# Pacing the side work of a fused attention and FFN kernel: due times for matmul units, lone VectorE score tiles, zero fillers

## The chip, the cores and the metric

The kernel runs on one core of a Trainium2 chip. The metric is the device time of one execution in microseconds (us). The kernel before has a median of 885.13 us in 3 runs.

## The reference

The input x is 2048 x 640 in bfloat16. It is normalized to xn, and the output is x plus attention of xn plus a squared-ReLU feed-forward network of xn. Attention has 32 heads of 20 columns for q, and one k and one v for all of them.

```python
xn = (x - mean(x)) / sqrt(var(x) + 1e-5)
q = (xn @ wq).reshape(B, S, 32, 20); k = xn @ wk; v = xn @ wv
p = softmax(einsum("bhqd,bkd->bhqk", q, k) * 20 ** -0.5)
a = einsum("bhqk,bkd->bhqd", p, v).reshape(B, S, 640) @ wo
h = relu(xn @ w1 + b1) ** 2
out = x + a + h @ w2 + b2
```

## The kernel before, in words

**Blocks and tiles.** An opening of some 30 us loads x, normalizes and transposes it (xnT) and makes the first keys, values and queries. Then come 32 blocks: 4 query chunks of 512 rows (qc) times 8 groups of 4 heads (g). A block has 64 score tiles, 16 key tiles (kt) times 4 heads, each of 128 keys x 512 queries in one PSUM bank. The 2048 tiles are shared between two engines.

**ScalarE's tiles (ACT).** PE computes a score step (make_step, line 806): 3 tiles, then 2, then 3 again, into banks 0 to 2 and 3 to 4. The 4 heads lie on 4 groups of 32 rows of the PE array, so the matmuls of a step are row-tiled and run side by side. ACT takes the exponential of a whole step with one ACTIVATE (line 840). When the 4 heads of a key tile are done, a PV group of 4 column-tiled matmuls multiplies them with v into bank 6 (make_pv, line 850). A step waits for the ACTIVATE two steps back, since it takes over its banks.

**VectorE's tiles (DVE).** A set is one key tile with its 4 heads (new_set, line 902, takes the last unclaimed key tile of the block). Each head's scores go into bank 5 (make_dqk, line 919). DVE turns them into a number whose bits approximate the exponential (D1, line 956) and, once per set, makes a correction with W, U, T1 and T2 (lines 963 to 974) on 128 x 2048 elements; T2 of every second set runs on POOL in two halves (line 972). U writes ubuf, of which there is one, so U of a set waits for T2 of the set before. Three PV groups per set follow (make_dpv, line 864). In the kernel before, PE computes such a tile only straight behind a score step, if the planner has it ready within 0.05 us then.

**Misc units.** The rest of PE's work is cut into units that share bank 7, each with an evacuation on DVE: unit_QT (queries of a block), unit_FFN1 (128 hidden columns of a query chunk; DVE adds the bias and takes the maximum, POOL squares), unit_OUT (128 rows x 320 columns of the output of a finished query chunk: 12 groups of the second FFN matmul, 1 of the bias, 8 of the out-projection), and unit_OUTP, the same for the last chunk without the last 2 head groups. Each step of a unit is a group of 4 column-tiled matmuls (col4, line 576). The list misc (lines 744 to 771) gives their order.

**The planner.** The order on every engine is fixed while the program is built (the loop at lines 993 to 1106). It knows a planned duration and the inputs of each operation, and takes again and again the one that can start first; among those that start within 0.03 us the lower number of priority goes first: on PE 0 for a score step, 1 for PV, 2 for a misc unit. A misc unit is taken from the first six of the list as soon as its inputs are planned (lines 1037 to 1042). On the chip each engine works its list in this order and waits for semaphores. The planner keeps DVE's double-speed operations and POOL's apart in time (lock).

**The end.** After the loop PE adds the last two head groups for the last chunk (tail_mm, line 1118), DVE adds the stored part (tail_ev, line 1127), and SP stores the rows.

Of the kernel before, what the change touches and what calls it, by code (L numbers as in the profile page):

```python
# [37 lines left out]
DLEAD = 14.0  # L38

# [49 lines left out]
class Op:  # L89
# [3 lines left out]
    def __init__(self, name, eng, dur, parts, deps=(), toks=(), lat=0.06, lock=False):  # L93
# [3 lines left out]
        self.lat, self.lock = lat, lock  # L97
# [14 lines left out]
def bass_parallel_sum__grouped_kv_mqa__dense_activation_squared_relu__prompt_kernel(nc, A_x, A_wq, A_wk, A_wv, A_wo, B_x, B_w1, B_b1, B_w2, B_b2, out):  # L112
    es = ExitStack()
    with es:
# [40 lines left out]
        part = sb("part", [128, 4, D], F32)  # L155
        scr = sb("scr", [128, 4], F32)
# [6 lines left out]
        ubuf = xfree[:, 4 * SETW:5 * SETW]  # L163
# [75 lines left out]
        v_vxpad = c_pool.n  # L239

# [349 lines left out]
        def unit_KT(c):  # L590
            sts = range(4 * c, 4 * c + 4)
            ch = [(0.21, (lambda dt=dt: col4(lambda j: wk_c[:, dt, :], xnT[:, dt, 512 * c:512 * (c + 1)], 512, dt, dt == DT - 1, DH))) for dt in range(DT)]
# [51 lines left out]
        def unit_FFN1(qc, f):  # L644
            sts = range(4 * qc, 4 * qc + 4)
            ch = [(0.21, (lambda dt=dt: col4(lambda j: w1_sb[:, dt, f * 128 + 32 * j:f * 128 + 32 * j + 32], xnT[:, dt, qc * 512:(qc + 1) * 512], 512, dt, dt == DT - 1)))
                  for dt in range(DT)]

            def evac(p):
# [11 lines left out]
                q = Op(f"SQ{qc}_{f}", "POOL", 1.05, [lambda e: e.tensor_tensor(out=h2T[:, qc % 2, f, :], in0=hT_tmp[:, k % 2, :], in1=hT_tmp[:, k % 2, :], op=ALU.mult)], dp, tk, lock=True)  # L661
# [20 lines left out]
        def out_chunks(mats, bank=MB, first=True, last=True):  # L682
            n = len(mats)
            ch = []
            for k, (l, r) in enumerate(mats):
                kk = k if first else k + 1
                ch.append((0.145, (lambda kk=kk, k=k, l=l, r=r: col4(lambda j: l[:, 32 * j:32 * j + 32], r, 320, kk, last and k == n - 1, 32, bank))))
# [39 lines left out]
        GP1 = G - 2  # L727
# [24 lines left out]
        misc.append(unit_B1())  # L752
        for qc in range(QC):
            ff = [unit_FFN1(qc, f) for f in range(FT)]
            oo = [unit_OUT(qc - 1, st, h) for st in range(4 * (qc - 1), 4 * qc) for h in range(2)] if qc >= 1 else []
            for g in range(G):
                b = qc * G + g
                if b + 2 < NBLK:
                    misc.append(unit_QT(b + 2))
                nf = min(2, len(ff)) if qc == QC - 1 else (FT * (g + 1)) // G - (FT * g) // G  # L760
                lst = ff[:nf]
                ff = ff[nf:]
                if qc < QC - 1:
                    misc += lst
                if oo:
                    misc.append(oo.pop(0))
                if qc == QC - 1:
                    misc += lst
        for st in range(4 * (QC - 1), ST):
            for h in range(2):  # L770
                misc.append(unit_OUTP(st, h))
# [34 lines left out]
        def make_step():  # L806
# [20 lines left out]
            st_["qk"] = Op(f"QK{j}", "PE", 0.31 if len(tl) < 3 else 0.33, parts, deps, toks, lat=0.2)  # L827
# [22 lines left out]
        def make_pv(b, kt):  # L850
# [11 lines left out]
            return Op(f"PV{b}_{kt}", "PE", 0.22, parts, deps, toks, lat=0.2)  # L862

        def make_dpv(s):
# [14 lines left out]
            return Op(f"DPV{b}_{kt}_{term}", "PE", 0.22, parts, deps, toks, lat=0.2)  # L879
# [39 lines left out]
        def make_dqk(heads):  # L919
# [16 lines left out]
            else:  # L936
                toks += all_pro
            return Op(f"DQK{d}", "PE", 0.06, [mm(ps[:, bank, :], kT[32 * h:32 * h + DH, kt * 128:(kt + 1) * 128], qT[32 * h:32 * h + DH, b % NQS, :], True, True, (32 * h, 0))],
                      deps, toks, lat=0.2), s, h, bank
# [7 lines left out]
        def after_dqk(o, s, h, bank):  # L947
# [8 lines left out]
            d1 = dv(f"D1_{n}_{i}", 0.66, lambda e: e.tensor_scalar(out=lbuf[:, a, cs].bitcast(U16), in0=ps[:, bank, :], scalar1=XA, scalar2=XB, op0=ALU.mult, op1=ALU.add),  # L956
# [36 lines left out]
        while True:  # L993
            best = {}

            def consider(eng, prio, op, ap):
# [5 lines left out]
                s = max(free[eng], r)  # L1002
                if op.lock:
                    s = max(s, lock_free[0])
                best.setdefault(eng, []).append((s, prio, op, ap))
# [57 lines left out]
            if pick is None:  # L1063
                break
            _, prio, o, ap = pick
# [52 lines left out]
        def tail_mm(k, g, first, last):  # L1118
# [4 lines left out]
            o = Op(f"OF{k}_{g}", "PE", 0.145, out_chunks(mats, bank, first, last)[0][1](), deps, lat=0.2)  # L1123
# [131 lines left out]
```

## Time and profile before

| | |
|---|---|
| median of 3 runs | 885.13 us (882.9 to 886.19) |
| the profiled execution's own time | 884.17 us |
| its span, first to last instruction | 882.4 us |
| busy: PE, DVE, ACT, POOL | 790.4, 658.4, 809.1, 251.3 us |
| mean granted clock of TensorE | 0.814 |

The median says how long the kernel takes; the rows of the trace all come from the one profiled execution, so sums are made against its 884.17 us, which is its span and 1.8 us around it. Busy time counts an engine's own instructions, and for PE the end of a matmul is modelled, since matmuls overlap. The granted clock is 1.0 at 2.4 GHz and 0.5 at 1.2 GHz.

### The profile page before, as it was taken

To read this page: it belongs to the slowest core of one execution; us is meant where nothing else is said; L and a number is where in the kernel's file an instruction comes from. 1 tells how busy PE (TensorE), PEld (TensorE's weight loads), DVE (VectorE), ACT (ScalarE), POOL (GpSimd) and SP (SyncE) were. 2 spreads that over 40 slices of the span, in tenths; PEclk is the share of its full clock that TensorE was granted. 3 is DMA by queue.
4 is the path that set the end of the run, shared out by engine and by line. 5 is a ranking of instruction groups with operands and counts; after the bars stand their busy time and mean duration, and the time that the engine had idled before them with its cause. 6 is when DMAs were issued, how large, how long until landed. Compare 5 with 4: busy or idle time off the path is not lost.

```text
span 882.4 us, 20648 instructions
## 1 busy us (share of the span) xinstructions
PE 790.4 (90%) x9319; PEld 239.7 (27%) x9319; DVE 658.4 (75%) x942; ACT 809.1 (92%) x732; POOL 251.3 (28%) x162
## 2 busy tenths in 40 slices
PE   7699988889899999988999989988889999978997
PEld 3222222111123333312114333321122333311333
DVE  6778887866668898886657887877586688875763
ACT  7599998998889999999889989999998999999895
POOL 3323433132113233522112332342121135221230
PEclk8689987655569999977559999986576999965799
DMA  9300000000000000000000000000000000000000
GB/s 322 84 1 2 1 1 1 1 1 1 1 2 16 17 16 3 16 1 1 1 1 16 18 1 17 16 2 1 1 1 1 17 17 17 16 1 1 2 2 32
DMA packets 11706, 14.81 MB, mean 17 GB/s; under 512 B 2017, under 2 KB 10978, under 8 KB 11618
## 3 DMA queue, kind: packets, MB, share of 16 engines
q1 hardware_dynamic: 10306, 13.44, 4.9%
q8 instruction: 73, 1.20, 0.5%
q10 hardware_dynamic: 1312, 0.05, 0.1%
q14 instruction: 15, 0.12, 0.0%
HBM read 10.87 MB, written 2.62 MB: 15 GB/s over the span
## 4 chain that ended last, share of the span: by engine, by line
PE 48%; ACT 42%; DVE 6%; issue 1%; DVEq 0%
PE ps L533 48%; ACT PT L840 42%; DVE x_sb L956 1%; DVE hT_tmp L652 1%; DVE Tn L890 1%; DVE qT L635 1%; DVE T L892 0%; DVE x_sb L965 0%; PE ps L581 0%; DVE out_sb L715 0%; DVE out_sb L1132 0%; DVE x_sb L963 0%; DVE part L734 0%; DVE OTn L896 0%; DVE tbuf L967 0%
## 5 line engine op out<-in xcount | busy, mean ns | idle before, releaser
L840 ACT ACTIVATE PT<-ps 128x1536 bf16<-128x1536 f32 (+1 forms) x685 | 788.6, 1265 | 57.1 <-PE ps L533 54.0
L533 PE MATMUL ps<-qT,kT 20*128 20x512 bf16 x2048 | 332.9, 458 | 63.2 <-ACT PT L840 55.2
L956 DVE TENSOR_SCALAR x_sb<-ps 128x512 uint16<-128x512 f32 x336 | 230.5, 686 | 140.8 <-PE ps L533 138.8
L972 POOL TENSOR_TENSOR tbuf<-tbuf,x_sb 128x1024 bf16<-128x1024 bf16 x84 | 178.8, 2151 | 435.5 <-DVE tbuf L967 435.5
L533 PE MATMUL ps<-PT,vx 128*32 128x512 bf16 x1712 | 201.6, 462 | 2.4 <-DVE Tn L890 2.4
L533 PEld LDWEIGHTS ps<-qT,kT 20*128 20x128 bf16 x2048 | 72.2, 94 | 343.5 <-ACT PT L840 251.5
L967 DVE TENSOR_TENSOR tbuf<-x_sb 128x2048 bf16<-128x2048 bf16 x84 | 103.7, 1235 | 1.4
L661 POOL TENSOR_TENSOR big<-hT_tmp 128x512 bf16<-128x512 bf16 x48 | 54.7, 1146 | 151.7 <-DVE hT_tmp L652 151.7
L533 PEld LDWEIGHTS ps<-PT,vx 128*32 128x32 bf16 x1712 | 45.0, 95 | 135.7 <-issue 129.0
L533 PE MATMUL ps<-xnT,w_sb 128*32 128x512 bf16 x960 | 74.8, 401 | 6.4 <-DVE qT L635 2.8
L533 PE MATMUL ps<-w_sb,big 128*32 128x320 bf16 x1536 | 75.5, 309 | 2.5 <-DVE part L734 0.8
L963 DVE TENSOR_SCALAR x_sb<-x_sb 128x2048 uint16<-128x2048 uint16 x84 | 69.3, 825 | 1.4
L965 DVE TENSOR_SCALAR x_sb<-x_sb 128x2048 uint16<-128x2048 uint16 x84 | 62.1, 740 | 0.0
L533 PE MATMUL ps<-xnT,wq_sb 128*20 128x512 bf16 x620 | 56.8, 473 | 1.1 <-DVE out_sb L715 0.6
L974 DVE TENSOR_TENSOR tbuf<-tbuf,x_sb 128x2048 bf16<-128x2048 bf16 x42 | 51.7, 1232 | 0.2
L533 PE MATMUL ps<-wo_pad,OTn 128*32 128x320 bf16 x1024 | 49.3, 300 | 0.7 <-DVE part L734 0.7
L533 PEld LDWEIGHTS ps<-w_sb,big 128*32 128x32 bf16 x1536 | 37.9, 98 | 28.5 <-issue 9.5
L652 DVE TENSOR_SCALAR hT_tmp<-ps,b1col 128x512 bf16<-128x512 f32 x48 | 35.8, 746 | 9.8 <-PE ps L533 8.8
L533 PE MATMUL ps<-x_sb,vx 128*32 128x512 bf16 x336 | 38.7, 450 | 2.6 <-DVE Tn L890 2.5
L533 PE MATMUL ps<-tbuf,vxc 128*32 128x512 bf16 x336 | 39.2, 456 | 0.3 <-POOL tbuf L972 0.2
L533 PE MATMUL ps<-x_sb,vxh 128*32 128x512 bf16 x336 | 38.8, 452 | 0.0
L635 DVE CAST qT<-ps 128x512 bf16<-128x512 f32 x31 | 21.2, 682 | 20.5 <-PE ps L533 20.2
(81 smaller groups left out, 315.2 us busy)
## 6 DMA issues: line engine op xcount, KB each, us to landing
w_sb<-in_B_w_dram SPq DMA_DIRECT2D x2, 1920.0 KB, 10.6
xr<-in_A_x_dram SPq DMA_DIRECT2D x16, 160.0 KB, 2.3
out_dram<-out_sb SPq DMA_DIRECT2D x16, 160.0 KB, 1.8
x_sb<-in_A_x_dram SPq DMA_DIRECT2D x3, 640.0 KB, 6.7
wq_sb<-in_A_wq_dram SPq DMA_DIRECT2D x1, 800.0 KB, 9.7
wo_pad<-in_A_wo_dram SPq DMA_DIRECT2D x4, 200.0 KB
x_sb<-in_A_x_dram SPq DMA_DIRECT2D x2, 320.0 KB, 3.5
wk_c<-in_A_wk_dram ACTq DMA_DIRECT2D x1, 25.0 KB, 3.2
```

Source lines behind the costliest of these rows:

```text
L533: return lambda e: e.matmul(out_, l, r, start=start, stop=stop, tile_position=tp)
L635: o = Op(f"QTe{b}", "DVE", 0.66, [lambda e: e.tensor_copy(out=qT[:, b % NQS, :], in_=ps[:, MB, :])], [p] + list(q_users.get(b - NQS, [])))
L652: o = Op(f"RL{qc}_{f}", "DVE", 0.75, [lambda e: e.tensor_scalar(out=hT_tmp[:, k % 2, :], in0=ps[:, MB, :], scalar1=b1col[:, f:f + 1], scal ...
L661: q = Op(f"SQ{qc}_{f}", "POOL", 1.05, [lambda e: e.tensor_tensor(out=h2T[:, qc % 2, f, :], in0=hT_tmp[:, k % 2, :], in1=hT_tmp[:, k % 2, : ...
L840: return Op(f"ACT{st_['j']}", "ACT", 0.064 + 0.4267 * n, [lambda e: e.activation(out=PT[:, s0:s0 + n, :], in_=ps[:, b0:b0 + n, :], func=AF ...
L890: tn = Op(f"TN{b}", "DVE", 0.72, [lambda e: e.transpose(out=Tn[:, a, :], in_=ps[:, PVB, :])], [lastpv, tm_op.get(b - 2)])
L956: d1 = dv(f"D1_{n}_{i}", 0.66, lambda e: e.tensor_scalar(out=lbuf[:, a, cs].bitcast(U16), in0=ps[:, bank, :], scalar1=XA, scalar2=XB, op0= ...
L963: s["wop"] = [dv(f"W{n}", 0.65, lambda e: e.tensor_scalar(out=W.bitcast(U16), in0=L.bitcast(U16), scalar1=0xFF80, scalar2=124, op0=ALU.bit ...
L965: s["uop"] = dv(f"U{n}", 0.65, lambda e: e.tensor_scalar(out=ubuf.bitcast(U16), in0=L.bitcast(U16), scalar1=0x7F, scalar2=0x3F80, op0=ALU. ...
L967: s["t1"] = [dv(f"T1_{n}", 1.17, lambda e: e.tensor_tensor(out=T, in0=L, in1=ubuf, op=ALU.mult), [s["uop"]] + ([("pv", old, 2)] if old els ...
L972: s["t2"].append(dv(f"T2_{n}", 2.1, lambda e, ks=ks: e.tensor_tensor(out=T[:, ks], in0=T[:, ks], in1=ubuf[:, ks], op=ALU.mult), s["t1"], 4 ...
L974: s["t2"].append(dv(f"T2_{n}", 1.17, lambda e: e.tensor_tensor(out=T, in0=T, in1=ubuf, op=ALU.mult), s["t1"], 4))
```

## The change

Units get a due time `at`, counted in blocks, and are taken only when the planner's progress has reached it: the opening's units at 0, the others spread by their cost over what is left of the 32 blocks, and QT of block b at b - 2 + 0.02. The planner charges 0.1 us when PE goes from row-tiled (mode R) to column-tiled (mode C) matmuls or back, and new durations: 0.215 us for a score step (0.31 to 0.33 before), for a PV and for each group of QT, KT and FFN1 (0.21 or 0.22 before), 0.14 for a group of OUT (0.145), 1.15 for a square (1.05). A DVE score tile may ride with a score step if it is ready within 0.1 us of it, and go alone if no score step can start within 0.5 us. While PE has a gap and has been planned busy for less than 0.7 of the time, it is given fillers: 4 matmuls with zero weights that add to bank 6. There are two ubufs, in a tensor of their own. OUTP leaves out 3 head groups instead of 2.

```diff
+DGAP = 0.5
+SWITCH = 0.1
+FILL = 0.7
...
+        zeros32 = sb("zeros32", [128, 32], BF16)
...
-        ubuf = xfree[:, 4 * SETW:5 * SETW]
+        ubuf = sb("ubuf", [128, 2, SETW], BF16)
...
+        add(P.pool, lambda e: e.memset(zeros32[:], 0.0), inc=c_pool)
+        v_zeros = c_pool.n
...
-        def commit(op):
-            s = max(free[op.eng], op.ready())
+        pe_mode = ["C"]
+
+        def start_of(op, r, switch=True):
+            s = max(free[op.eng], r)
+            if switch and op.eng == "PE" and op.mode != pe_mode[0]:
+                s = max(s, free["PE"] + SWITCH)
             if op.lock:
                 s = max(s, lock_free[0])
+            return s
+
+        def commit(op):
+            s = start_of(op, op.ready())
+            if op.eng == "PE":
+                pe_mode[0] = op.mode
...
-        GP1 = G - 2
+        GP1 = G - 3
...
+        for u in misc:
+            u.at = 0.0
+        others = []
         for qc in range(QC):
...
+            if qc == 0:
+                others += [(unit_FFN1(0, f), 0.3) for f in range(FT)] + [(unit_FFN1(1, f), 0.3) for f in range(FT)]
+            else:
+                others += [(unit_OUT(qc - 1, st, h), G * qc + 0.1) for st in range(4 * (qc - 1), 4 * qc) for h in range(2)]
+                if qc + 1 < QC:
+                    others += [(unit_FFN1(qc + 1, f), G * qc) for f in range(FT)]
+        others += [(unit_OUTP(st, h), NBLK - (G - GP1) + 0.1) for st in range(4 * (QC - 1), ST) for h in range(2)]
+        cost = [sum(c[0] for c in u.chunks) for u, _ in others]
+
+        left = sum(cost)
+        t = 0.3
+        for (u, t0), c in zip(others, cost):
+            t = max(t, t0)
+            u.at = t
+            t += c * (NBLK - 0.3 - t) / left
+            left -= c
+        for b in range(2, NBLK):
+            q = unit_QT(b)
+            q.at = b - 2 + 0.02
+            others.append((q, 0.0))
+        misc += [u for u, _ in sorted(others, key=lambda x: x[0].at)]
...
-            return Op(f"DQK{d}", "PE", 0.06, [mm(
+            return Op(f"DQK{d}", "PE", 0.02 if heads else 0.215, [mm(
...
-            s["uop"] = dv(f"U{n}", 0.65,
-                          s["d1"] + (sets[n - 1]["t2"] if n >= 1 else []), 4, True, x_read if n < 1 else ())
+            s["uop"] = dv(f"U{n}", 0.74,
+                          s["d1"] + (old["t2"] if old else []), 4, True, x_read if n < 2 else ())
...
+        credit = [0.0, 0.0]
+
+        def pe_credit(t):
+            credit[1] = min(credit[1] - FILL * (t - credit[0]), 0.6)
+            credit[0] = t
+            return credit[1]
...
-                if rd is not None and rd <= free["PE"] + 0.05:
+                if rd is not None and heads[0] and rd <= free["PE"] + 0.1:
                     best["PE"] = [(max(free["PE"], rd), -1, r[0], ("dqk",) + r[1:])]
                 else:
-                    heads[0] = None
+                    heads[0] = []
+                    if r is not None:
+                        r[0].dur = 0.215
+                    nq = pend[0]["qk"].ready() if pend[0] is not None else None
+                    if rd is not None and (nq is None or nq > max(free["PE"], rd) + DGAP):
+                        consider("PE", 3, r[0], ("dqk",) + r[1:])
...
+                progress = cur["b"] + 1.0 - len(unclaimed[cur["b"]]) / KT
                 for u in misc[:6]:
-                    if u.can():
+                    if u.at <= progress and u.can():
...
+            if pick[2].eng == "PE":
+                while pick[0] > free["PE"] + 0.1 + (0.2 if pick[2].mode == "R" and pe_mode[0] == "R" else 0.0) and pv_blk[0] < NBLK and pv_blk[0] in pv_begun and pe_credit(free["PE"]) < 0.0:
+                    f_ = Op("fill", "PE", 0.215, [mm(ps[32 * jj:32 * jj + 32, PVB, :], zeros32[:, :], kT[:, 0:512], False, False, (0, 32 * jj)) for jj in range(4)])
+                    commit(f_)
+                    credit[1] += f_.dur
+                pe_credit(max(pick[0], free["PE"]))
+                credit[1] += pick[2].dur
...
-            tail_mm(k, G - 2, True, False)
+            for g in range(GP1, G - 1):
+                tail_mm(k, g, g == GP1, False)
```

The planned durations of D1, W, U and T1 go from 0.66, 0.65, 0.65 and 1.17 to 0.686, 0.74, 0.74 and 1.235 us, of T2 from 1.17 to 1.235 (2.1 to 2.15 for a half on POOL).

## Rows read from the trace of the kernel before

**Rows 1.** The page: busy times, granted clock in 40 slices, chain that ended last.
```profile
PE 790.4 (90%) x9319; PEld 239.7 (27%) x9319; DVE 658.4 (75%) x942; ACT 809.1 (92%) x732; POOL 251.3 (28%) x162
...
PEclk8689987655569999977559999986576999965799
...
PE 48%; ACT 42%; DVE 6%; issue 1%; DVEq 0%
```

**Rows 2.** Stretches: us, busy (count) of PE, PEld, DVE, ACT, POOL; granted clock, DMA.
```profile
60.00:120.00 60.00, 54.65 (x686) 16.01 (x690) 52.81 (x73) 59.44 (x53) 22.93 (x17) 1.00 0.01 2
120.00:280.00 160.00, 142.16 (x1237) 34.06 (x1229) 114.34 (x155) 141.15 (x123) 39.04 (x21) 0.66 0.01 2
280.00:380.00 100.00, 92.94 (x1397) 33.08 (x1395) 88.10 (x122) 99.35 (x88) 37.14 (x22) 1.00 0.04 13
380.00:480.00 100.00, 90.16 (x828) 22.21 (x824) 64.45 (x92) 91.89 (x81) 23.11 (x12) 0.66 0.00 1
480.00:580.00 100.00, 91.96 (x1365) 31.90 (x1357) 85.24 (x118) 96.43 (x85) 32.47 (x19) 0.98 0.05 15
580.00:680.00 100.00, 89.06 (x775) 20.84 (x771) 72.11 (x100) 90.54 (x79) 25.17 (x14) 0.66 0.00 1
680.00:780.00 100.00, 93.35 (x1423) 33.76 (x1419) 81.29 (x116) 98.43 (x86) 30.24 (x18) 0.98 0.05 15
780.00:840.00 60.00, 54.50 (x491) 13.34 (x487) 39.22 (x54) 55.60 (x49) 13.30 (x7) 0.60 0.00 1
840.00:872.00 32.00, 30.47 (x553) 13.06 (x553) 14.59 (x23) 31.34 (x28) 5.46 (x3) 1.00 0.01 3
...
40.00:872.00 832.00, 758.18 (x8920) 224.00 (x8920) 624.93 (x865) 781.77 (x680) 234.14 (x134) 0.81 0.02 6
```

**Rows 3.** Groups by line, 280 to 380 us: count, busy us, mean ns, idle before.
```profile
L956 DVE TENSOR_SCALAR x_sb<-ps 128x512 uint16<-128x512 f32 x46 | 31.5, 685 | 7.2 <-PE ps L533 7.0
...
L533 PE MATMUL ps<-PT,vx 128*32 128x512 bf16 x220 | 22.0, 389 | 0.8 <-DVE Tn L890 0.8
```

**Rows 4.** The same view, 190 to 230 us.
```profile
L533 PE MATMUL ps<-PT,vx 128*32 128x512 bf16 x72 | 11.1, 607 | 0.3 <-DVE Tn L890 0.3
L956 DVE TENSOR_SCALAR x_sb<-ps 128x512 uint16<-128x512 f32 x14 | 9.6, 689 | 10.3 <-PE ps L533 10.1
```

**Rows 5.** Groups of the whole span, from the page.
```profile
L840 ACT ACTIVATE PT<-ps 128x1536 bf16<-128x1536 f32 (+1 forms) x685 | 788.6, 1265 | 57.1 <-PE ps L533 54.0
...
L956 DVE TENSOR_SCALAR x_sb<-ps 128x512 uint16<-128x512 f32 x336 | 230.5, 686 | 140.8 <-PE ps L533 138.8
...
L967 DVE TENSOR_TENSOR tbuf<-x_sb 128x2048 bf16<-128x2048 bf16 x84 | 103.7, 1235 | 1.4
...
L963 DVE TENSOR_SCALAR x_sb<-x_sb 128x2048 uint16<-128x2048 uint16 x84 | 69.3, 825 | 1.4
L965 DVE TENSOR_SCALAR x_sb<-x_sb 128x2048 uint16<-128x2048 uint16 x84 | 62.1, 740 | 0.0
```

**Rows 6.** Timeline of PE: start us, length us, instructions merged.
```profile
80.45 1.26 PE L533 MATMUL ps<-xnT,w_sb 128*32 128x512 bf16 x20
81.64 0.39 PE L533 MATMUL ps<-qT,kT 20*128 20x512 bf16 x3
81.96 0.40 PE L533 MATMUL ps<-PT,vx 128*32 128x512 bf16 x4
...
855.29 1.13 PE L533 MATMUL ps<-w_sb,big 128*32 128x320 bf16 x28
```

**Rows 7.** Instructions on tile hT_tmp: ns min/median/max, first and last start.
```profile
L248 PE MATMUL ps<-hT_tmp,ones_bf x22: 379/380/634, 1.5 to 8.0; 128*128 128x512 bf16 x22
```

**Rows 8.** Timeline of POOL in the opening.
```profile
9.57 1.74 POOL L301 TENSOR_SCALAR big<-x_sb,rstd,nmr 128x640 bf16<-128x640 bf16 x2 [6.52 <-DVE nmr L294]
```

**Rows 9.** Timeline of the end.
```profile
875.07 0.45 DVE L734 TENSOR_TENSOR part<-ps,xr 128x320 f32<-128x320 f32 x1
...
876.90 3.28 DVE L1132 TENSOR_TENSOR out_sb<-ps,part 128x320 bf16<-128x320 f32 x8 [1.38 <-PE ps L533]
```

More of the change, by code (lines that the diff above doesn't have):

```diff
@@ L89, with __init__ @@
 class Op:
-    def __init__(self, name, eng, dur, parts, deps=(), toks=(), lat=0.06, lock=False):
+    def __init__(self, name, eng, dur, parts, deps=(), toks=(), lat=0.06, lock=False, mode="C"):
         self.name, self.eng, self.dur, self.parts = name, eng, dur, parts
@@ L96, in __init__ @@
         self.toks = list(toks)
-        self.lat, self.lock = lat, lock
+        self.lat, self.lock, self.mode = lat, lock, mode
         self.start = self.fin = None
@@ L591, in unit_KT @@
             sts = range(4 * c, 4 * c + 4)
-            ch = [(0.21, (lambda dt=dt: col4(lambda j: wk_c[:, dt, :], xnT[:, dt, 512 * c:512 * (c + 1)], 512, dt, dt == DT - 1, DH))) for dt in range(DT)]
+            ch = [(0.215, (lambda dt=dt: col4(lambda j: wk_c[:, dt, :], xnT[:, dt, 512 * c:512 * (c + 1)], 512, dt, dt == DT - 1, DH))) for dt in range(DT)]
             def evac(p):
@@ L660, in evac @@
                     dp += dp2
-                q = Op(f"SQ{qc}_{f}", "POOL", 1.05, [lambda e: e.tensor_tensor(out=h2T[:, qc % 2, f, :], in0=hT_tmp[:, k % 2, :], in1=hT_tmp[:, k % 2, :], op=ALU.mult)], dp, tk, lock=True)
+                q = Op(f"SQ{qc}_{f}", "POOL", 1.15, [lambda e: e.tensor_tensor(out=h2T[:, qc % 2, f, :], in0=hT_tmp[:, k % 2, :], in1=hT_tmp[:, k % 2, :], op=ALU.mult)], dp, tk, lock=True)
                 ffn_sq.append(q)
@@ L686, in out_chunks @@
                 kk = k if first else k + 1
-                ch.append((0.145, (lambda kk=kk, k=k, l=l, r=r: col4(lambda j: l[:, 32 * j:32 * j + 32], r, 320, kk, last and k == n - 1, 32, bank))))
+                ch.append((0.14, (lambda kk=kk, k=k, l=l, r=r: col4(lambda j: l[:, 32 * j:32 * j + 32], r, 320, kk, last and k == n - 1, 32, bank))))
             return ch
@@ L752, in bass_parallel_sum__grouped_kv_mqa__dense_activation_squared_relu__prompt_kernel @@
         misc.append(unit_B1())
+        for u in misc:
+            u.at = 0.0
+        others = []
         for qc in range(QC):
[L754 to L771, printed above, removed]
+            if qc == 0:
[18 more added lines that the diff above has]
+        misc += [u for u, _ in sorted(others, key=lambda x: x[0].at)]
         unclaimed = [list(range(KT)) for _ in range(NBLK)]
@@ L826, in make_step @@
                 toks += all_pro
-            st_["qk"] = Op(f"QK{j}", "PE", 0.31 if len(tl) < 3 else 0.33, parts, deps, toks, lat=0.2)
+            st_["qk"] = Op(f"QK{j}", "PE", 0.215, parts, deps, toks, lat=0.2, mode="R")
             for (b, kt, h) in tl:
@@ L937, in make_dqk @@
                 toks += all_pro
-            return Op(f"DQK{d}", "PE", 0.06, [mm(ps[:, bank, :], kT[32 * h:32 * h + DH, kt * 128:(kt + 1) * 128], qT[32 * h:32 * h + DH, b % NQS, :], True, True, (32 * h, 0))],
-                      deps, toks, lat=0.2), s, h, bank
+            return Op(f"DQK{d}", "PE", 0.02 if heads else 0.215, [mm(ps[:, bank, :], kT[32 * h:32 * h + DH, kt * 128:(kt + 1) * 128], qT[32 * h:32 * h + DH, b % NQS, :], True, True, (32 * h, 0))],
+                      deps, toks, lat=0.2, mode="R"), s, h, bank
         def dv(name, dur, fn, deps, prio, lock=True, toks=(), eng="DVE"):
@@ L955, in after_dqk @@
             old = sets[n - 2] if n >= 2 else None
-            d1 = dv(f"D1_{n}_{i}", 0.66, lambda e: e.tensor_scalar(out=lbuf[:, a, cs].bitcast(U16), in0=ps[:, bank, :], scalar1=XA, scalar2=XB, op0=ALU.mult, op1=ALU.add),
+            d1 = dv(f"D1_{n}_{i}", 0.686, lambda e: e.tensor_scalar(out=lbuf[:, a, cs].bitcast(U16), in0=ps[:, bank, :], scalar1=XA, scalar2=XB, op0=ALU.mult, op1=ALU.add),
                     [o] + ([old["pv"][0], old["t1"][0], old["uop"], old["wop"][0]] if old else []), 1, False, x_read if n < 2 else ())
@@ L1001, in consider @@
                     return
[L1002 to L1005, printed above, removed]
+                best.setdefault(eng, []).append((start_of(op, r, False), prio, op, ap))
             if act_next < len(steps) and steps[act_next]["qk"].fin is not None and act_can(steps[act_next]):
@@ L1122, in tail_mm @@
             deps = [tb_op[(qc, g)], part_ev[(st, h)]] + (bank_free[bank] if first else [])
-            o = Op(f"OF{k}_{g}", "PE", 0.145, out_chunks(mats, bank, first, last)[0][1](), deps, lat=0.2)
+            o = Op(f"OF{k}_{g}", "PE", 0.14, out_chunks(mats, bank, first, last)[0][1](), deps, lat=0.2)
             commit(o)
@@ L1141, in bass_parallel_sum__grouped_kv_mqa__dense_activation_squared_relu__prompt_kernel @@
         for k in range(7):
-            tail_mm(k, G - 2, True, False)
+            for g in range(GP1, G - 1):
+                tail_mm(k, g, g == GP1, False)
         for k in range(8):
             if k == 7:
-                tail_mm(k, G - 2, True, False)
+                for g in range(GP1, G - 1):
+                    tail_mm(k, g, g == GP1, False)
             p = tail_mm(k, G - 1, False, True)
```

22 lines of the change are left out of this document (11 added, 11 removed).

## The prediction

> **What bounds the kernel now.** The page first. ScalarE (ACT) is busy 92% of the span and PE 90%, and the chain that ended last is made of these two, 48% and 42%. PE's share is modelled, so the next thing to see is the line of the granted clock: it is not steady, it swings four times between 9 and 5 tenths [rows 1].
>
> The stretches show what the swing means. In four of them (60 to 120, 280 to 380, 480 to 580, 680 to 780 us, 360 us together) the clock is 0.98 to 1.00, that is 2.4 GHz, and PE has some 11 to 14 matmuls per us. ACT is idle there for 0.56, 0.65, 3.57 and 1.57 us, 6.35 us or 1.8%. In the four between (420 us) the clock averages 0.60 to 0.66 with about 8 matmuls per us, and ACT is idle for 18.85, 8.11, 9.46 and 4.40 us, 40.82 us or 9.7% [rows 2]. That is 41 of all 57.1 us that line 840 sat idle, nearly all of it until a PE matmul ended [rows 5].
>
> The groups of one dense and one thin stretch show why: a PV matmul takes 389 ns in the first and 607 in the second, which is the same work at 1.2 GHz [rows 3, 4]. What differs is the misc units. The list is taken greedily, so the out-projection and FFN1 units of a query chunk are used up in its first half, and the second half has little but score and PV matmuls. PE does less per us, the clock falls, and what is left takes so long that ACT waits.
>
> VectorE (DVE) has room: 624.93 of the 832 us from 40 to 872, but 88.10 of 100 in the best dense stretch [rows 2]. It waits most before L956, the first step of a score tile: 7.2 us of 100 in the dense stretch, 10.3 of 40 in the thin one, both for PE [rows 3, 4]. So ACT bounds the dense stretches, and PE at the low clock delays ACT in the thin ones.
>
> **The sum, part by part**, against the profiled execution's own 884.17 us, 0.96 under the median of the runs.
>
> A. **Pacing and fillers keep the clock up.** FFN1, OUT and OUTP units, and QT from block 2, get due times spread by cost over the 32 blocks. Four kinds of work are moved with them: their matmuls, evacuations on DVE, the squares on POOL, and the loads and stores on SP; each slot has blocks, not us, before its next use, so nothing waits for them. If the thin 420 us idle like the dense 360, their 40.82 us become 7.4: **-33.4**. Bounds: 0 if the clock does as before, -42 if all 780 us idle like 280 to 380 (0.65%). I take 1.8% because the new mix is nearest to the four dense stretches together.
>
> The PE load supports this. A column-tiled group of 4 matmuls costs 0.215 us at the high clock: five take 1.26, the last 0.40, so four starts cover 0.86. A 320-column group costs (1.13 - 0.175) / 7 = 0.137, the 0.175 being what one group outlasts its slot (0.39 - 0.215). After a score step the next mode starts 0.32 us on, 0.105 over the slot [rows 6]. With 672 score steps, 420 PV, 276 DVE-PV, 155 QT, 10 KT and 240 FFN1 groups (counts from the loops, with 8 more sets, below), 672 of the 320-column ones and, an assumption, 120 score tiles that go alone: 1893 x 0.215 + 672 x 0.137 = 499 us. Two switches for each of 792 row-tiled steps are 166. Fillers, to 0.7 of 782 us, add 48, about 225 of them. That is 713 of 782 us, 91%. The stretch 280 to 380, by the same account (88 score steps with 265 matmuls, 163 groups of 512 columns and 120 of 320, which make its 1397 matmuls [rows 2]), has 37 + 35 + 16 = 89%, and ACT idles 0.65% there. I take **0** for the fillers; bounds 0 and, if a quarter of the 225 delay ACT by a whole slot, +12.
>
> Do fillers with zero weights count for the clock? The warm-up matmuls have a moving operand of zeros, and among those 22 the length falls from 634 to 380 ns [rows 7]. So I take it that zeros count.
>
> B. **More DVE sets.** A set of 4 tiles costs DVE 4 x 0.686 + 0.825 + 0.740 + 1.235 and half as much again of a T2 like T1, together 6.16 us, and spares ACT 4 x 788.6 / 1712 = 1.84 us, the 1712 being 2048 less the 336 of L956 [rows 5]. A score tile may now go alone when the next step is over 0.5 us off, and the second ubuf frees U from the T2 of the set before, which POOL may still be working on. I take the best dense share, 0.881, from 40 to 790 us, with the last 32 us before the end as they are (14.59): 661 against 624.93 - 14.59 = 610 [rows 2], 51 us more, 8 sets: **-14.7**. Bounds: the planner charges 6.1 us for a set where it charged 5.7, so in the same planned time 5 sets fewer, +9; DVE at 0.95, 16 sets more, -30. Each D-PV group is counted above; L956 takes the bank before PE can refill it, as now.
>
> C. **The end.** The last part is evacuated at 875.07, and only then do the last 64 out-projection matmuls run, with the first result at 876.90 [rows 9]. OUTP units are now due from 3 blocks before the end, and lack one group more. Groups 5 and 6 are then ready while DVE normalizes the last block, and behind OTn, which DVE has done just before 875.07, stand only 0.14 of matmul, its latency (some 0.4) and the evacuations, so the first comes at about 875.6: **-1.3**. Bounds: +1.1 (8 groups more in line) and -2.
>
> D. **The rest at 0.** The memset of zeros32 on POOL lies in the 6.52 us that POOL waits for nmr [rows 8]; without that cover it is less than one of the two operations of that row, 0.9 us. Planner durations alter only the order. The wait moved to the older T2 is met earlier, so what stands behind U on DVE comes no later.
>
> Sum: 884.17 - 33.4 - 14.7 - 1.3 = 834.8, and with the 0.96 to the median **836 us**. What is late next is ACT itself, nearly full.
>
> **The rule on switching.** In rows 6 PV starts 0.32 us after the score step, whose matmuls are recorded for 0.39: the next mode starts before the former has ended, and a switch costs 0.105. The Trainium skill (TensorEngine Tiling (Array Packing), section Tiling Modes) says that changing the tiling mode drains TensorE. A full drain would by that rule cost 0.175 here, PE would need 547 + 1584 x 0.175 = 824 us where the sum above leaves 782, and the sum would be 42 higher, 877. This trace doesn't agree at this place.
>
> **Rivals.**
>
> 1. *Clock held, no more sets.* For it: line 956 may be held by the POOL lock and by the order, and the planner charges more per set. Against it: the waits for PE. 884.17 - 33.4 - 1.3 = 850, up to 859 with 5 sets fewer.
>
> 2. *The clock falls where no unit is due.* The due times leave blocks of about 6.0 to 8.1, 15.5 to 16.1, 23.2 to 24.1 and 28.2 to 29.1 without FFN or OUT work, some 4.5 blocks of 26 us. If fillers don't do there, ACT idles in these 117 us like the worst thin stretch (18.85 of 160 us, 11.8% [rows 2]) and not 1.8%: +12, so 848. For it: in the thin stretches QT units alone did not hold the clock. Against it: rows 7, and that PE is filled to 70% there.
>
> 3. *Fillers make PE the bound: slower.* The place is the gap between two score steps, where a filler adds its slot and two changes of mode. From the 499 + 48 us of slots, 1584 switches and up to 450 more, PE needs more than today's 832 us if a switch costs over 0.140. With half of the fillers so placed and 0.175 each, 547 + 1809 x 0.175 = 864, 32 more than now: about 916. For it: the 91%. Against it: 0.105 in rows 6, and that a filler is placed only where the plan has a gap and PE is behind its 70%. By the skill's rule above this rival would be the likeliest; the row speaks against it.
>
> 4. *The units do not spread.* Six units are looked at, each also needs its inputs; if due times pass while they wait, they bunch again and it stays at 884. Against it: inputs are ready blocks ahead.
>
> **How the numbers follow.** Forecast 0.63, rival 1 0.13, rival 2 0.12, rival 3 0.07, rival 4 0.05. The forecast's own range is 817 to 858 (A from -42 to -22, B from -26 to 0, not all at one end). With rivals 1 and 2 inside, 814 to 866 holds 8 in 10. Half a percent (4 us) is what a measurement here can tell from no change. Faster by more: 0.63 + 0.13 + 0.12, less some 0.02 for mishaps, 0.86; within it 0.06; slower 0.08.
>
> **What would show it.** In the new profile: the clock line without fives after 60 us, PV matmuls near 390 ns in every stretch, L840's idle near 24 us instead of 57; L956 some 368 times; ACT over 98% busy from 60 to 780. The last evacuation group should start about 2.5 us after the last PV. The prediction is wrong if fives stay in the blocks without units, if ACT idles before PE matmuls at the high clock (rival 3), or if L956 comes 336 times or fewer (rival 1).

## The result and the profile after

The changed kernel takes 838.03 us (median of 4 runs, 831.29 to 843.30) against 885.54 before: a ratio of 0.9465, 95% interval 0.9377 to 0.9553. The forecast was 836 with a range of 814 to 866. The profiled execution took 842.64 us with a span of 840.8, against 884.17 and 882.4.

The page of the changed kernel: busy times, granted clock and the chain that ended last, which answer to [rows 1].

```profile
PE 775.6 (92%) x10439; PEld 254.9 (30%) x10439; DVE 678.5 (81%) x973; ACT 794.5 (94%) x724; POOL 268.4 (32%) x168
...
PEclk8689999987989999999999999999999999999999
...
ACT 61%; PE 28%; DVE 6%; issue 1%; DVEq 0%
```

The clock has no fives after the opening, and the chain is now 61% ACT and 28% PE, where it was 42% and 48%. The groups of the same page (count | busy us, mean ns | idle before) answer to [rows 5]. Line 862 is the exponential, 840 before; 978 is D1, 956 before; the third is new: the fillers, below also called zero groups, 272 groups of 4 matmuls.

```profile
L862 ACT ACTIVATE PT<-ps 128x1536 bf16<-128x1536 f32 (+1 forms) x679 | 775.0, 1294 | 29.3 <-PE ps L549 27.5
...
L978 DVE TENSOR_SCALAR x_sb<-ps 128x512 uint16<-128x512 f32 x352 | 241.3, 685 | 113.2 <-PE ps L549 110.7
...
L549 PE MATMUL ps<-kT,zeros 128*32 128x512 bf16 x1088 | 87.9, 401 | 0.0
```

ACT's idle time before an exponential falls from 57.1 to 29.3 us, its busy time there from 788.6 to 775.0, and there are 352 D1 instead of 336, that is 88 sets. The stretches (us, busy of PE, PEld, DVE, ACT, POOL, clock) answer to [rows 2]; here one that was dense before, 280 to 380, and three that were thin, and then two from a second cut.

```profile
120.00:280.00 160.00, 149.99 (x1822) 43.74 (x1810) 125.81 (x172) 148.37 (x130) 52.62 (x30) 0.91 0.01 4
280.00:380.00 100.00, 93.38 (x1363) 31.82 (x1358) 84.95 (x119) 99.24 (x88) 29.09 (x15) 1.00 0.04 12
380.00:480.00 100.00, 92.68 (x1239) 29.34 (x1237) 84.46 (x115) 97.11 (x86) 34.34 (x19) 0.98 0.02 5
...
580.00:680.00 100.00, 93.81 (x1299) 30.01 (x1291) 85.77 (x119) 96.38 (x87) 34.97 (x20) 1.00 0.02 5
```

```profile
60.00:180.00 120.00, 112.96 (x1411) 32.88 (x1403) 101.32 (x141) 119.81 (x106) 48.05 (x33) 1.00 0.01 2
180.00:260.00 80.00, 75.44 (x821) 20.47 (x824) 58.05 (x79) 69.75 (x61) 22.00 (x11) 0.83 0.01 2
```

From 280 to 380 us ACT idles 0.76 us, as before. The stretch 380 to 480 lost 8.11 before and 2.89 now, 580 to 680 lost 9.46 and 3.62. The exception is 180 to 260: ACT idles 10.25 of 80 us there at a clock of 0.83. These are blocks 6 to 8, the longest part without FFN or OUT units: from 179.2 to 254.4 us the trace has no matmul of either. The same cut for the zero groups alone shows 64 of the 272 in these 80 us:

```profile
60.00:180.00 120.00, 8.02 (x96) 2.26 (x96) 0.00 (x0) 1.00 0.01 2
180.00:260.00 80.00, 22.84 (x256) 6.83 (x256) 0.00 (x0) 0.83 0.01 2
```

In this execution they were not enough. The timeline of PE shows the clock going down among them: two zero groups take 0.60 us at 182.28, three take 1.51 from 183.59 (at the high clock three take 0.82, as at 827.67), and the score step behind them takes 0.61 where 0.39 is the length at the high clock.

```profile
182.28 0.60 PE L549 MATMUL ps<-kT,zeros 128*32 128x512 bf16 x8
182.82 0.52 PE L549 MATMUL ps<-qT,kT 20*128 20x512 bf16 x3
...
183.59 1.51 PE L549 MATMUL ps<-kT,zeros 128*32 128x512 bf16 x12
185.03 0.61 PE L549 MATMUL ps<-qT,kT 20*128 20x512 bf16 x3
```

The end, which answers to [rows 9]: the last block's first DVE operation (L912), and the first of the last evacuations.

```profile
832.37 0.72 DVE L912 STREAM_TRANSPOSE Tn<-ps 128x512 f32<-128x512 f32 x1 [6.78 <-PE ps L549]
...
835.28 3.28 DVE L1171 TENSOR_TENSOR out_sb<-ps,part 128x320 bf16<-128x320 f32 x8 [0.43 <-PE ps L549]
```

From one to the other it takes 2.91 us. Before, the same operation, L890, started at 872.67 and the first of the last evacuations, L1132, at 876.90 [rows 9], 4.23 us.

```profile
872.67 0.72 DVE L890 STREAM_TRANSPOSE Tn<-ps 128x512 f32<-128x512 f32 x1 [0.78 <-PE ps L533]
```

### The profile page after: what moved, and what is told of

Read it like the earlier page. It is cut to its first block, busy times and chain, and to the rows that moved or that the text cites. A ratio compares the mean times of both kernels' runs of the same rounds, so it can differ in the third digit from the quotient of the medians.

```text
span 840.8 us, 22953 instructions
## 1 busy us (share of the span) xinstructions
PE 775.6 (92%) x10439; PEld 254.9 (30%) x10439; DVE 678.5 (81%) x973; ACT 794.5 (94%) x724; POOL 268.4 (32%) x168
## 4 chain that ended last, share of the span: by engine, by line
ACT 61%; PE 28%; DVE 6%; issue 1%; DVEq 0%
ACT PT L862 61%; PE ps L549 28%; DVE x_sb L978 2%; DVE tbuf L989 1%; DVE T L914 1%; DVE ubuf L987 1%; DVE x_sb L985 0%; DVE hT_tmp L668 0%; PE ps L597 0%; DVE out_sb L1171 0%; DVE Tn L912 0%; DVE qT L651 0%; DVE kT L611 0%; DVE OTn L918 0%; PE ps L624 0%
## 5 line engine op out<-in xcount | busy, mean ns | idle before, releaser
L862 ACT ACTIVATE PT<-ps 128x1536 bf16<-128x1536 f32 (+1 forms) x679 | 775.0, 1294 | 29.3 <-PE ps L549 27.5
L549 PE MATMUL ps<-qT,kT 20*128 20x512 bf16 x2048 | 309.7, 393 | 46.3 <-ACT PT L862 33.1
L994 POOL TENSOR_TENSOR tbuf<-tbuf,ubuf 128x1024 bf16<-128x1024 bf16 x88 | 191.6, 2197 | 448.5 <-DVE tbuf L989 448.5
L978 DVE TENSOR_SCALAR x_sb<-ps 128x512 uint16<-128x512 f32 x352 | 241.3, 685 | 113.2 <-PE ps L549 110.7
L549 PE MATMUL ps<-PT,vx 128*32 128x512 bf16 x1696 | 171.1, 397 | 3.3 <-DVE Tn L912 3.1
L989 DVE TENSOR_TENSOR tbuf<-x_sb,ubuf 128x2048 bf16<-128x2048 bf16 x88 | 113.4, 1289 | 0.6
L549 PE MATMUL ps<-kT,zeros 128*32 128x512 bf16 x1088 | 87.9, 401 | 0.0
L985 DVE TENSOR_SCALAR x_sb<-x_sb 128x2048 uint16<-128x2048 uint16 x88 | 68.6, 780 | 0.5
L987 DVE TENSOR_SCALAR ubuf<-x_sb 128x2048 uint16<-128x2048 uint16 x88 | 66.4, 755 | 0.0
L996 DVE TENSOR_TENSOR tbuf<-tbuf,ubuf 128x2048 bf16<-128x2048 bf16 x44 | 55.5, 1261 | 0.0
```

What stands on the lines that cost most here:

```text
L549: return lambda e: e.matmul(out_, l, r, start=start, stop=stop, tile_position=tp)
L862: return Op(f"ACT{st_['j']}", "ACT", 0.064 + 0.4267 * n, [lambda e: e.activation(out=PT[:, s0:s0 + n, :], in_=ps[:, b0:b0 + n, :], func=AF ...
L978: d1 = dv(f"D1_{n}_{i}", 0.686, lambda e: e.tensor_scalar(out=lbuf[:, a, cs].bitcast(U16), in0=ps[:, bank, :], scalar1=XA, scalar2=XB, op0 ...
L985: s["wop"] = [dv(f"W{n}", 0.74, lambda e: e.tensor_scalar(out=W.bitcast(U16), in0=L.bitcast(U16), scalar1=0xFF80, scalar2=124, op0=ALU.bit ...
L987: s["uop"] = dv(f"U{n}", 0.74, lambda e: e.tensor_scalar(out=ubuf[:, a, :].bitcast(U16), in0=L.bitcast(U16), scalar1=0x7F, scalar2=0x3F80, ...
L989: s["t1"] = [dv(f"T1_{n}", 1.235, lambda e: e.tensor_tensor(out=T, in0=L, in1=ubuf[:, a, :], op=ALU.mult), [s["uop"]] + ([("pv", old, 2)] ...
```

## The experiments

All of them start from the changed kernel. Ratios are to the kernel before on the same chip, with 95% intervals. The order of the opening comes from iterating over a Python set and so differs from build to build; in all twelve it is fixed.

**e1, the changed kernel with a fixed opening**

```diff
-            unsched = set(tasks.keys())
+            unsched = dict.fromkeys(tasks)
...
-                unsched.discard(n)
+                unsched.pop(n, None)
```

> The changed kernel, with the order of the opening made the same in every build. All theories: 831 to 843 us, as the changed kernel's own runs. If the spread of those runs came from the opening's order, the rounds of this one lie within 3 us of each other; if it comes from where the clock happens to fall, they spread over 8 us or more.

833.13 us (829.53 to 835.26), ratio 0.9367 (0.9325 to 0.9408). The spread of 5.7 us lies between what the two readings asked, so it stays open how much of the 12 us between the changed kernel's executions comes from the opening. There the time goes with the clock: 831.29 and 833.43 us at a mean of 0.981 and 0.976, 842.64 and 843.30 at 0.962 and 0.965. In e1's profile the first exponential starts at 28.67 us, against 31.78 in the changed kernel's and 31.44 before. The clock is low after the opening for 6.8 us from 234.6, and for 3.4 us each at 333.5 and 412.1.

```profile
PEclk8789999999989999999999999999999999999999
...
ACT 63%; PE 26%; DVE 6%; issue 1%; DVEq 0%
```

```profile
L862 ACT ACTIVATE PT<-ps 128x1536 bf16<-128x1536 f32 (+1 forms) x679 | 774.1, 1301 | 19.9 <-PE ps L549 18.2
...
L549 PE MATMUL ps<-PT,vx 128*32 128x512 bf16 x1696 | 169.3, 393 | 3.2 <-DVE Tn L912 3.1
```

PV matmuls have a mean of 393 ns, against 462 before; 389 is the high clock and 607 the low [rows 3, 4]. This row is the yardstick for the others. The line of the kernel before:

```profile
L533 PE MATMUL ps<-PT,vx 128*32 128x512 bf16 x1712 | 201.6, 462 | 2.4 <-DVE Tn L890 2.4
```

The part without FFN and OUT units lies here from 175.6 to 242.8 us. Between 184 and 235 us the clock stays at 1.00, with 52 zero groups, and ACT idles 0.11 of 51 us. So the same plan can hold the clock in this place or lose it.

```profile
184.00:235.00 51.00, 46.78 (x580) 13.46 (x572) 44.75 (x60) 50.89 (x45) 13.00 (x6) 1.00 0.01 2
```

**e2, the same plan without the zero groups; e3, pacing undone; e8, both.** In e2 and e8 the list of the filler's matmuls is empty; in e3 and e8 the units come in the old order with a due time of 0. e3 has 292 zero groups, e1 272.

```diff
-                    f_ = Op("fill", "PE", 0.215, [mm(ps[32 * jj:32 * jj + 32, PVB, :], zeros32[:, :], kT[:, 0:512], False, False, (0, 32 * jj)) for jj in range(4)])
+                    f_ = Op("fill", "PE", 0.215, [])
```

> The same plan, order and sets as e1, but the 272 zero groups are not issued. Theory that the fillers hold the clock where no unit is due: PV matmuls at 600 ns in the blocks without units, ACT idle up by 8 to 15 us, 845 to 853 us. Rival, units and DVE tiles alone hold the clock: PV near 390 ns in the same places as in e1 and the time of e1 or up to 5 us less, since 58 us of PE slots are gone.

> Pacing undone: units in the old order, taken as soon as they can be, OUTP one block earlier than before; fillers, durations, lone tiles and two ubufs stay. Theory that pacing is the main part: the thin halves come back, the clock falls there though fillers are planned, 855 to 875 us. Rival, fillers alone hold the clock: 832 to 845 us, with some 250 to 500 filler groups, nearly all in the second halves of the chunks.

> Pacing undone as in e3, and no zero group is issued. What is left of the change: planned durations, mode switch in the plan, lone tiles, two ubufs, OUTP earlier. Theory that nearly all of the gain comes through the clock: 870 to 886 us, and the clock falls in the second half of each chunk as before. Rival, the better plan is worth much by itself: 850 to 868 us.

| | without fillers | with fillers |
|---|---|---|
| old order of units | e8: 876.58 us, 0.9885 (0.9840 to 0.9929) | e3: 848.10 us, 0.9539 (0.9502 to 0.9577) |
| paced units | e2: 883.09 us, 0.9931 (0.9879 to 0.9982) | e1: 833.13 us, 0.9367 (0.9325 to 0.9408) |

The pages of e2, e3 and e8, in this order:

```profile
PEclk8799999865569589899865997899976999857998
...
L862 ACT ACTIVATE PT<-ps 128x1536 bf16<-128x1536 f32 (+1 forms) x679 | 781.0, 1281 | 70.1 <-PE ps L549 67.4
...
L549 PE MATMUL ps<-PT,vx 128*32 128x512 bf16 x1696 | 190.8, 444 | 3.6 <-DVE Tn L912 3.3
```

```profile
L860 ACT ACTIVATE PT<-ps 128x1536 bf16<-128x1536 f32 (+1 forms) x679 | 777.3, 1274 | 29.8 <-PE ps L549 27.7
...
L549 PE MATMUL ps<-PT,vx 128*32 128x512 bf16 x1696 | 170.8, 396 | 3.6 <-DVE Tn L910 3.5
```

```profile
PEclk8799997655569999986567999997577999985999
...
L860 ACT ACTIVATE PT<-ps 128x1536 bf16<-128x1536 f32 (+1 forms) x679 | 781.0, 1263 | 58.2 <-PE ps L549 55.9
```

Without fillers pacing gains nothing: e2's clock falls in many places, not only where no unit is due, and ACT idles 70.1 us, more than before (this profiled execution took 889.46 us, 6 above its median, so 70.1 is more than usual). In the ten executions of e2 the mean clock is 0.824 to 0.861, in the four of e1 0.972 to 0.981. From 184 to 235 us, where e1 had the clock at 1.00 with its zero groups, e2 has 0.53:

```profile
184.00:235.00 51.00, 47.31 (x310) 9.19 (x310) 36.07 (x52) 42.40 (x37) 9.70 (x5) 0.53 0.00 1
```

So the theory for e2 had the right sign and was far too small, and its rival falls. Fillers alone do most: e3 has a PV mean of 396 ns. Neither of e3's two forecasts holds, it lies between them; pacing adds 15 us to the fillers. e8 says what the rest of the change is worth: 1.2%, some 10 us, inside what its first theory had.

**e4, due times without unit-free blocks**

```diff
-        left = sum(cost)
-        t = 0.3
...
+        seg_a = [0.3, G + 0.1, 2 * G + 0.1, 3 * G + 0.1, NBLK - (G - GP1) + 0.1]
+        seg_z = [G, 2 * G, 3 * G, NBLK - (G - GP1), NBLK - 0.3]
+        seg_n = [2 * FT, 8 + FT, 8 + FT, 8, 8]
...
+                others[k][0].at = t
+                t += cost[k] * (z_ - a_) / whole
```

> Due times spread evenly inside each span between two releases (0.3 to 8, 8.1 to 16, and so on), so that no blocks are without FFN1 or OUT units. Theory that the loss at 180 to 260 us (10 us of ACT idle, low clock) belongs to the unit-free blocks 6 to 8: no PV matmul at 600 ns after 60 us, ACT idle from 29 to about 19 us, 826 to 833 us. Rival, the clock falls by chance wherever PE is at 0.7: the same time as e1 within 3 us, with a fall somewhere else.

862.60 us, ratio 0.9665 (0.9589 to 0.9740), with 252 zero groups: worse than e1 by 29 us, and both expectations fall.

```profile
PEclk8699999699999899999999989989998998899999
...
L867 ACT ACTIVATE PT<-ps 128x1536 bf16<-128x1536 f32 (+1 forms) x679 | 779.0, 1276 | 47.5 <-PE ps L549 45.8
...
L549 PE MATMUL ps<-PT,vx 128*32 128x512 bf16 x1696 | 176.1, 408 | 1.7 <-DVE Tn L917 1.7
```

The clock now falls a little in many places. What is shown is that taking the unit-free blocks away does not cure the falls. That the even spread leaves no stretch as dense as those of e1 is an argument only.

**e5, each filler doubled; e6 and e12, PE filled to 0.8 and 0.75**

```diff
-                    f_ = Op("fill", "PE", 0.215, [mm(... ) for jj in range(4)])
+                    f_ = Op("fill", "PE", 0.215, [mm(... ) for _ in range(2) for jj in range(4)])
```

```diff
-FILL = 0.7
+FILL = 0.8
```

> The plan, order and sets of e1, but each of the 272 filler places issues two zero groups; the planner does not know of the second, so PE gets 272 x 0.215 = 58 us of slots more. Theory that fillers lie in gaps: the added time is below 12 us and the clock holds everywhere, 828 to 845 us. Rival, fillers stand in front of score steps and PE is near its bound: half to all of the 58 us reaches ACT, 862 to 891 us, at the high clock.

> e1 with the share to which PE is filled at 0.8 and not 0.7. Theory that 0.7 is marginal, and that units above it keep the clock up elsewhere: no PV matmul near 600 ns after 60 us, ACT idle from 19.9 to 12 to 16 us, 822 to 831 us. Rival, what fillers win in clock they lose in front of score steps: 833 to 850 us, with ACT idle up at the high clock.

> e1 with PE filled to 0.75: 416 zero groups instead of 272, 348 D1. Theory that the best share lies where the clock just holds, and that each group beyond it costs ACT up to 0.15 us (e5: 40 us for 272): between e1 and e6, 836 to 848 us, with cold PV matmuls for under 20 us after 60 us. Rival, 0.7 is still below the best and the last falls of the clock cost more than the 144 groups: 822 to 832 us, faster than both kernels.

e5: 873.40 us, ratio 0.9850 (0.9806 to 0.9894). e6: 851.60, 0.9581 (0.9525 to 0.9637). e12: 850.83, 0.9636 (0.9594 to 0.9678). The pages of e5 and e6 (busy times, clock, chain, groups):

```profile
PE 812.8 (93%) x11527; PEld 281.4 (32%) x11527; DVE 672.7 (77%) x972; ACT 803.6 (92%) x726; POOL 266.4 (31%) x167
...
PE 49%; ACT 41%; DVE 5%; issue 1%; DVEq 0%
...
L862 ACT ACTIVATE PT<-ps 128x1536 bf16<-128x1536 f32 (+1 forms) x679 | 783.2, 1260 | 51.0 <-PE ps L549 46.9
...
L549 PE MATMUL ps<-PT,vx 128*32 128x512 bf16 x1696 | 169.0, 392 | 3.7 <-DVE Tn L912 3.5
```

```profile
PE 819.2 (96%) x11567; PEld 275.8 (32%) x11567; DVE 682.2 (80%) x972; ACT 802.9 (94%) x726; POOL 268.8 (32%) x167
...
PE 83%; DVE 7%; ACT 7%; issue 0%; DVEq 0%
...
L862 ACT ACTIVATE PT<-ps 128x1536 bf16<-128x1536 f32 (+1 forms) x679 | 782.5, 1251 | 32.1 <-PE ps L549 28.9
```

In e5 the clock is as high as in e1 (392 ns), yet the span grows from 831.0 to 870.0: 39 us for 272 groups that the planner did not know of, 0.143 us each of a slot of 0.215. So the rival of e5 holds: a group more reaches ACT for two thirds. For groups that are planned no run gives a price of one alone, since each number of them makes another plan. In e6 554 groups are planned, and PE is the bound: 96% busy and 83% of the chain. The window 40 to 840 us of e6 shows it once more:

```profile
40.00:840.00 800.00, 784.94 (x11164) 260.19 (x11156) 648.67 (x893) 771.98 (x671) 251.35 (x138) 0.99 0.02 7
```

By the account of the prediction e6 needs 499 + 166 + 554 x 0.215 = 784 us of PE there, and it was busy 784.94. But this nearness is partly luck: the 166 is for 1584 changes between row-tiled and column-tiled matmuls, and e6's trace has 1413, which at 0.105 make 148 and a need of 766. The 0.105 itself holds: the median from the start of a score group to that of the column-tiled group behind it is 0.320 us in e6, and back from a group of 512 columns 0.322, each 0.105 to 0.107 over the slot of 0.215. e12, with 416 groups and one set fewer than e1 (348 D1), lands beside e6, above what was expected, at nearly e1's clock (0.965 to 0.981) and with 51% PE in its chain against 26%; 0.7 is better than both.

**e9, PE filled to 0.6; e10, fillers of half the columns**

```diff
-FILL = 0.7
+FILL = 0.6
```

```diff
-                    f_ = Op("fill", "PE", 0.215, [mm(ps[32 * jj:32 * jj + 32, PVB, :], zeros32[:, :], kT[:, 0:512], False, False, (0, 32 * jj)) for jj in range(4)])
+                    f_ = Op("fill", "PE", 0.215, [mm(ps[32 * jj:32 * jj + 32, PVB, 0:256], zeros32[:, :], kT[:, 0:256], False, False, (0, 32 * jj)) for jj in range(4)])
```

> e1 with PE filled to 0.6: 113 zero groups instead of 272 and the same 352 D1. Theory that the clock needs the 272: the clock falls in the blocks without units and elsewhere, cold PV matmuls for over 80 us, 845 to 865 us, between e2 and e1. Rival, most of the 272 only cost PE slots: 822 to 832 us and the clock as in e1.

> The plan, order and sets of e1, each of the 272 zero groups with 256 columns instead of 512, so half its slot. Theory that the planned fillers cost nothing on ACT's path and the clock needs them: the clock falls more often, 840 to 860 us. Rival, planned fillers cost what the doubled ones of e5 did (40 of 58 us): 29 us of slots fewer bring up to 20 us, 813 to 828 us, with the clock nearly as in e1.

e9: 874.13 us, ratio 0.9889 (0.9851 to 0.9927). e10: 869.02 us, with runs from 848.39 to 881.62, too far apart for an interval, beside 883.51 for the kernel before.

```profile
L862 ACT ACTIVATE PT<-ps 128x1536 bf16<-128x1536 f32 (+1 forms) x679 | 779.0, 1289 | 56.4 <-PE ps L549 54.5
...
L549 PE MATMUL ps<-PT,vx 128*32 128x512 bf16 x1696 | 181.7, 423 | 1.3 <-DVE Tn L912 1.3
```

```profile
L549 PE MATMUL ps<-PT,vx 128*32 128x512 bf16 x1696 | 180.8, 420 | 3.6 <-DVE Tn L912 3.3
```

Both have the clock falling (PV 423 and 420 ns), and both are slower than e1 by more than their first theory said, e10 by its median; their rivals fall. With e5, e6 and e12 the zero groups have a narrow best among the numbers tried: fewer or shorter ones lose the clock, more of them load PE.

**e7, DVE tiles as before**

```diff
-                          s["d1"] + (old["t2"] if old else []), 4, True, x_read if n < 2 else ())
+                          s["d1"] + (sets[n - 1]["t2"] if n >= 1 else []), 4, True, x_read if n < 2 else ())
...
-            if heads[0] is not None:
+            if heads[0]:
...
-                if rd is not None and heads[0] and rd <= free["PE"] + 0.1:
+                if rd is not None and heads[0] and rd <= free["PE"] + 0.05:
...
-                    nq = pend[0]["qk"].ready() if pend[0] is not None else None
-                    if rd is not None and (nq is None or nq > max(free["PE"], rd) + DGAP):
-                        consider("PE", 3, r[0], ("dqk",) + r[1:])
+                    heads[0] = None
```

> e1 with the DVE tiles as before: only straight behind a score step, ready within 0.05 us, and U waiting for T2 of the set before. Theory that these two give the added sets: 336 D1 or fewer, and 84 sets, ACT busy up by 7 us, 839 to 845 us. Rival, the sets are bound by DVE and the lock and not by PE's order: 352 D1 again and 830 to 836 us.

841.15 us, ratio 0.9486 (0.9421 to 0.9552), 8 us more than e1.

```profile
L862 ACT ACTIVATE PT<-ps 128x1536 bf16<-128x1536 f32 (+1 forms) x685 | 781.6, 1288 | 23.6 <-PE ps L549 22.3
...
L978 DVE TENSOR_SCALAR x_sb<-ps 128x512 uint16<-128x512 f32 x336 | 230.8, 687 | 127.3 <-PE ps L549 124.1
```

336 D1, the 84 sets of before, and ACT busy 7.5 us longer than in e1 (781.6 against 774.1), with 314 zero groups: the lone tiles and the second ubuf together give the 4 sets; which of the two gives more stays open.

**e11, sets nearer to a block's end**

```diff
-DLEAD = 14.0
+DLEAD = 9.0
```

> e1 with DLEAD 9 instead of 14, so sets are claimed until 9 us before a block's tiles run out: 368 D1, 92 sets, 360 zero groups. Theory that ACT bounds and each set spares it 1.84 us: 7 us less than e1, 822 to 830 us. Rival, with more DVE groups and fillers PE is the bound: 833 to 848 us, ACT idle above 30 us at the high clock.

889.11 us, ratio 1.0059 (1.0013 to 1.0106): 0.6% slower than before, though ACT's exponentials are down to 771.6 us. Neither theory foresaw it. The exponential's group of the page, and the timeline around 120 us:

```profile
L862 ACT ACTIVATE PT<-ps 128x1536 bf16<-128x1536 f32 (+1 forms) x672 | 771.6, 1271 | 66.6 <-PE ps L549 64.5
```

```profile
121.32 0.40 PE L549 MATMUL ps<-tbuf,vxc 128*32 128x512 bf16 x4 [0.74 <-POOL tbuf L994]
121.77 0.72 DVE L912 STREAM_TRANSPOSE Tn<-ps 128x512 f32<-128x512 f32 x1
...
122.54 1.26 PE L549 MATMUL ps<-PT,vx 128*32 128x512 bf16 x20 [0.82 <-DVE Tn L912]
...
122.99 4.62 ACT L862 ACTIVATE PT<-ps 128x1536 bf16<-128x1536 f32 x4 [7.54 <-PE ps L549]
```

At a block's end PE waits for POOL's T2 of a set claimed late, then for L912 to empty bank 6, and behind these waits stand the score steps: ACT sits idle for 7.54 us. Over the whole trace 35.9 of the 66.6 us lie in seven waits of this kind, of 2.3 to 8.9 us within 1.5 us behind an L912; e1 has one, of 2.9 us. More sets are no use where their last PV group comes after the block's other tiles.

No run beats the changed kernel: e1 is the same plan, and its interval overlaps.

## Why the prediction was right, step by step

**The sum.** On the profiled executions the span fell by 41.6 us, where the steps made 49.4; the median fell by 47.5. Of the 41.6 ACT's idle time made 27.8, its busy time 13.6 and the end 1.3, together 42.7, 1.1 too many.

**A, the clock.** -33.4 was forecast, all of it idle time of ACT. That fell by 27.8 us (57.1 to 29.3). ACT's busy time fell by 13.6, of which the 16 tiles of the 4 new sets are 16 x 0.4606 = 7.4. The other 6.2 the prediction did not have. They go with the number of ACT's waits and not with the clock itself: the same 679 exponentials are busy for 774.1 us in e1 with 45 waits, 781.0 in e2 with 119, and 783.2 in e5 with 128, at the high clock. The changed kernel has 59, the kernel before 115. The records of exponentials overlap when none waits (before, 685 with a mean of 1265 ns are 867 us, busy 788.6 [rows 5]), so each wait lengthens the busy time too. With the 6.2 the step gave 34.0. That it came so near is partly luck: the prediction took pacing and fillers as one, and its reading of the thin halves named the misc units as the cause. The two by two table says that fillers carry the step, that pacing alone gives nothing, and that it adds 15 us to the fillers.

**The fillers at 0.** 272 came where 225 were counted. PE was not the bound with them (28% of the chain, in e1 26%), which fits the 0; no run shows it by itself, since without them the clock falls. The bound of +12 was too narrow for what lies beyond: one unplanned group more costs 0.143 us (e5), and the 91% of the account is nearer to the limit than the 89% of the dense stretch made it look. The switch price of 0.105 us from rows 6 held, but not the number of switches: 1584 were counted, and the changed kernel's trace has 1347.

**B, the sets.** This is the term that was mis-sized: 8 sets and -14.7 were forecast, 4 came and gave 16 x 0.4606 = 7.4. DVE was to be as busy as in the best dense stretch, 88%, and was busy 646.14 of the 790 us from 40 to 830, 82%; D1 still waits 110.7 us for PE in the changed kernel, against 138.8. That it waits because a lone tile goes only when no score step is near is an argument, which no run tests; e11 shows that easing the rule that ends a block's sets from 14 to 9 us does not help.

```profile
40.00:830.00 790.00, 741.57 (x10059) 239.52 (x10059) 646.14 (x896) 766.65 (x672) 250.34 (x138) 0.97 0.02 7
```

**C, the end.** -1.3 forecast, 4.23 - 2.91 = 1.32 measured. The sign beside it was wrong: the first of the last evacuations starts 3.36 us behind the start of the last PV (831.92), not 2.5, while the prediction's own 875.6 lies 3.37 behind that of before (872.23).

**Rival 1**, the clock held without more sets, was half true. **Rival 2** came true in one of its four places, blocks 6 to 8, and there not in every execution: ACT idled 10.25 of 80 us, against 1.4 at 1.8%, so it cost some 9 us, and in e1 the clock held there until 235 us. The place is longer than the prediction had it, 75 us where 2.1 blocks of 26 us are 55. Without fillers it would not have been 848, as priced, but 883 (e2): the clock does not fall in the unit-free blocks alone. **Rival 3**, the slower side, did not decide here, but PE can become the bound: it did in e6, by the number of groups and not by a switch of over 0.140. The rule of the Trainium skill that stood beside it (TensorEngine Tiling (Array Packing), section Tiling Modes) says that a mode change drains TensorE. With the 0.175 us of a full drain e6 would need 499 + 1413 x 0.175 + 119 = 865 us in a stretch of 800, so the trace does not agree. **Rival 4** did not occur.

**The other signs.** The clock line has no fives after 60 us, as named. PV matmuls were not near 390 ns in every stretch: from 180 to 260 us their mean is 439. The exponential's idle time is 29.3 us and not 24, D1 comes 352 times and not 368, and ACT is busy 97.2% from 60 to 780 us (699.80 of 720) and not over 98%.

## What to carry to other kernels

When ACT waits for PE, look at the granted clock and the length of one matmul by stretch before PE's busy share: here PE was some 90% busy at either clock. Work that keeps a clock up must be tried in more and in less: here the changed kernel gained 1% with none and with 113 zero groups, 6% with 272, 4% with 416. Spreading useful work evenly is not the same as keeping the engine loaded; alone it gave nothing here.

## What the runs showed of the hardware that was not expected

Matmuls with zero weights, whose results change nothing, can hold TensorE's clock at 2.4 GHz: the same plan takes 833 us with them, at a mean granted clock of 0.972 to 0.981, and 883 without, at 0.824 to 0.861. They do not always do it: in the changed kernel the clock falls among them at 183 us. At half the columns they do so less well (869 us). And evener work can lose the clock more often than uneven work: e4 falls from 0.977 to 0.938 in mean granted clock with nearly the same number of zero groups (252 and 272) as e1.
